# Three token tiles fed together while the weights are decoded, between 24 attention heads and the rest

## The chip, the cores and the metric

The kernel runs on one core of a Trainium2 chip. The metric is the device time of one execution in microseconds. Before the change its median is 1111.67 us over 3 runs (1111.55 to 1111.82).

The core has five engines that work side by side, each through a queue of its own in order: TensorE (PE in the profile: matrix products and transposes, results in the PSUM banks), VectorE (DVE), ScalarE (ACT), GpSimd (POOL) and SyncE (SP, which issues most of the transfers). PEld is TensorE's loading of stationary operands.

## The reference

An attention with a window and 32 global tokens, then a feed-forward layer over all 4608 tokens of the result (8 batches, 8 heads, 512 local and 32 global tokens each, 64 values per head). `sm` is a softmax.

```python
s_g = scale * q_g @ [k_g, k_l].T
out_g = sm(s_g) @ [v_g, v_l]                 # global queries see all keys
s_ll = where(|i - j| <= 32, scale * q_l @ k_l.T, -1e9)
s_lg = scale * q_l @ k_g.T
out_l = sm([s_lg, s_ll]) @ [v_g, v_l]        # local queries: window and global keys
x = concat([out_g, out_l]).reshape(4608, 512)
g = s * relu(x @ w_in) ** 2 + b              # w_in 512 x 2048
return (g @ w_out).astype(float32)           # w_out 2048 x 512
```

`w_in` and `w_out` reach the kernel as float64.

## The kernel before

**Attention** is cut into 128 slots `j`, one for each batch, half of its 512 queries, and head; I call a slot a head. A head has scores (`ps_s`), the scores of the global queries (`ps_g`), a softmax on VectorE, ScalarE and, for some, GpSimd, four transposes (`ps_t`) and the products with the values (`ps_o`). Each of these four PSUM tiles has one bank. Eight heads fill one tile `x` of 256 tokens. The heads 0 to `NF` - 1 are *plain*: float32 operands as they are (`scores32`, `transposes32`, `pv32`). The others are *split*: ScalarE makes a rounded high part, VectorE or GpSimd the low part, and TensorE works on float32r pairs (`split`, `scores`, `pv_products`). The global queries go by groups of four heads (`g_softmax`, `g_transposes`, `g_load`, `g_pv`).

**The feed-forward layer** runs over 17 tiles of 256 tokens (the last has the global ones, by way of DRAM). `x_split` or `xg_split` makes a tile's high and low part, `xs`. A tile has 8 *units*, each with two of the 16 columns of blocks of `w_in`. A unit's first products (`ffn_in`, L494: 24 of 128x256) go to a bank `ps_h`; ScalarE and VectorE make `r` and then `g` in high and low part (L500, L501, L508, L509); its second products (`ffn_out`, L526: 12 of 128x512) are added up over the tile's 8 units in two banks, `acc0` and `acc1`.

**The weights** come in 32 pieces, `w_in` and `w_out` in turn: `weight_piece` puts the words of the float64 together on VectorE (L129, L134, L138, L142), ScalarE (L132, L133, L145) and GpSimd (L144, L146), and leaves a high and a low part in SBUF for good. Unit `pr` of any tile needs the pieces 4 `pr` to 4 `pr` + 3. The list `SPOTS` says in whose buffers a piece is prepared, since no space is kept for it.

**The order** of the work is written out in one loop over `j`: loads for head `j` + 2, up to three weight pieces (`PIECES`, the 32 of them in the first 14 rounds), the scores of head `j`, the first products of unit `m` = `j` - `LAG` with `LAG` = 12, transposes of head `j` - 1 and values of `j` - 2, then the second products of unit `m` - 1. So each slot has one head and one unit, from unit 0 beside head 12; the last 20 slots have units alone or nearly so. A scheduler then places each engine's instructions by this order and by its own times; on the chip each engine keeps that order. With `NF` = 16 the plain heads are those of the first batch.

Of the kernel before, what the change touches and what calls it, by code (L numbers as in the profile page):

```python
# [20 lines left out]
P = 128  # L21
# [27 lines left out]
NORM_POOL = lambda j: j < NF  # L49
# [6 lines left out]
GL_POOL = lambda m: False  # L56
# [9 lines left out]
def window_attention_then_ffn(ctx: ExitStack, tc: tile.TileContext, qd, qg, kw, vw, vg, w_in, w_out, sv, bv, out):  # L66
# [33 lines left out]
    # The weights come as float64: a piece's words are put together as float32, with the exponent  # L100
    # bounded to float32's range (smaller is 0, larger not finite) and the mantissa rounded.
# [3 lines left out]
    def weight_piece(k):  # L105
# [22 lines left out]
        # 2^e with the sign  # L128
# [8 lines left out]
        # 1 + the mantissa: 8 + 20 bits of the high word, less 7, and the low word  # L137
# [54 lines left out]
    def softmax(j, p_s):  # L192
# [45 lines left out]
    def load32(j):  # L238
        b, hf, h = slot(j)
        if h % 2 == 0:  # L240
            if j % 4 == 0:
                rk = sb.tile([P, 480], F32, tag="rk", name=f"rk{j}", bufs=1)
            else:
                rk = sb.tile([P, 10 * D], F32, tag="rvg", name=f"rk{j}", bufs=1)[:, 0:480]
# [41 lines left out]
    # yields after each block's transposes  # L286
# [38 lines left out]
    def qg_load32(b):  # L325
        n = (NF - 16 * b) * SG
# [11 lines left out]
    def scores(j):  # L338
# [14 lines left out]
        # rows of the global queries: qh.k + ql.k  # L353
# [13 lines left out]
    # yields after each block's products  # L367
# [22 lines left out]
    # The last products of a block are shorter than the load of the next values' chunk: transposes go between.  # L390
# [39 lines left out]
    # by pairs of heads  # L430
# [27 lines left out]
    NT = 17  # L458
    xs_ = {}

    def x_split(t):
        xs = sb.tile([P, 2, 4, HALF], F32R, tag="xs", name=f"xs{t}", bufs=1)
        x = xcur.pop(t)
        for i in range(2):
            v = slice(2 * i, 2 * i + 2)
            nc.scalar.copy(out=xs[:, 0, v, :], in_=x[:, v, :])
            nc.vector.tensor_sub(out=xs[:, 1, v, :], in0=x[:, v, :], in1=f32(xs[:, 0, v, :]))
        xs_[t] = xs

    def xg_split(t):  # L470
        xs = sb.tile([P, 2, 4, HALF], F32R, tag="xs", name=f"xs{t}", bufs=1)
        for i in range(2):
# [12 lines left out]
    def ffn_in(m):  # L485
        t, pr = m // 8, m % 8
        xs = xs_[t]
        p_h = ps.tile([P, 2, HALF], F32, tag="h", name=f"ps_h{m}", bufs=2)
        for k in range(2):
            f = 2 * pr + k  # L490
            n = 0
            for c in range(4):
                for a, e in ((0, 0), (0, 1), (1, 0)):
                    nc.tensor.matmul(  # L494
                        p_h[:, k], lhsT=wi[:, a, c, f * P:(f + 1) * P], rhs=xs[:, e, c, :],
# [3 lines left out]
        r = sb.tile([P, 2, HALF], F32, tag="r", name=f"r{m}", bufs=2)  # L499
        nc.scalar.activation(out=r, in_=p_h, func=AF.Relu)  # L500
        nc.vector.scalar_tensor_tensor(out=r, in0=p_h, scalar=s_t, in1=r, op0=ALU.mult, op1=ALU.mult)  # L501
        g = sb.tile([P, 2, 2, HALF], F32R, tag="g", name=f"g{m}")
        if GL_POOL(m):
            nc.vector.tensor_scalar_add(r, r, b_t)
            nc.scalar.copy(out=g[:, 0], in_=r)
            nc.gpsimd.tensor_sub(out=g[:, 1], in0=r, in1=f32(g[:, 0]))
        else:
            nc.scalar.activation(out=g[:, 0], in_=r, func=AF.Identity, bias=b_t)  # L508
            nc.vector.scalar_tensor_tensor(  # L509
                out=g[:, 1], in0=r, scalar=b_t, in1=f32(g[:, 0]), op0=ALU.add, op1=ALU.subtract,  # L510
            )
        gs_[m] = g
# [3 lines left out]
    def ffn_out(m):  # L516
        t, pr = m // 8, m % 8
        g = gs_.pop(m)
        if pr == 0:
            oacc[t] = [ps.tile([P, DM], F32, tag=f"acc{i}", name=f"acc{t}_{i}") for i in range(2)]  # L520
# [25 lines left out]
    NM = NT * 8  # L546
# [12 lines left out]
    def pick(f32_one, split_one):  # L559
        def run(j):  # L560
            if NF <= j < NS:
                split_one(j)
            elif 0 <= j < NF:
                with tc.high_priority(offset=AHEAD):
                    f32_one(j)
        return run

    ld = pick(load32, load)
    sp = pick(lambda j: None, split)
    vl, vl32 = pick(lambda j: None, v_load), pick(v_load32, lambda j: None)  # L570
    sc = pick(scores32, scores)
    tr = pick(transposes32, lambda j: None)
    vsp = pick(lambda j: None, v_split)
    pvs = pick(pv32, lambda j: None)
    piece = 0
# [116 lines left out]
```

## Time and profile before

| | |
|---|---|
| median of 3 runs | 1111.67 us |
| span of the profiled execution, first to last instruction | 1109.8 us |
| time outside the span, median less span | 1.9 us |
| TensorE busy | 1064.7 us, 96% of the span |
| VectorE | 872.3 us, 79% |
| ScalarE | 722.4 us, 65% |
| GpSimd | 426.9 us, 38% |
| transfers | 86.80 MB, 78 GB/s on average |

Of the profiled execution the profile gives the span and no time of its own; the median of the runs stands in for it. The page cuts the span into 40 slices of 27.7 us and gives each engine's busy share in tenths. Timelines give the start and length of instructions in a row; since products overlap in the array, the distance from one start to the next is what a group costs, not its length. The granted clock is the share of TensorE's full clock.

### The profile page before, as it was taken

How to read it: one execution, taken by the hardware profiler on the slowest of the kernel's cores; microseconds unless marked ns; L12 is line 12 of the kernel's file. 1: busy time of each engine (PE TensorE's matmuls, PEld its weight loads, DVE VectorE, ACT ScalarE, POOL GpSimd, SP SyncE). 2: the span in 40 equal slices, each digit the busy share in tenths (PEclk: the TensorE clock that was granted, in tenths of full speed). 3: DMA queues.
4: the chain of work that ended last, by engine and by line, in shares of the span. 5: the costliest groups of instructions: out<-in, count | busy, mean ns of one | idle time of the engine just before them, and what ended most of it. 6: DMA issues, size and time to landing. Idle time of an engine off the chain costs nothing.

```text
span 1109.8 us, 20489 instructions
## 1 busy us (share of the span) xinstructions
PE 1064.7 (96%) x7048; PEld 930.7 (84%) x7048; DVE 872.3 (79%) x2119; ACT 722.4 (65%) x1828; POOL 426.9 (38%) x457
## 2 busy tenths in 40 slices
PE   4889879999999999999999999999999999999996
PEld 2457668889989889898998999989989899998885
DVE  7999998789778977798778977897789777964221
ACT  6666767677667766686767775776678676844221
POOL 6887774343224423343323433442344242411000
PEclk9968999999999999999999999999999999999998
DMA  6454422232213212231223221321223121201000
GB/s 231 149 164 140 153 67 87 69 95 72 63 50 93 77 37 93 66 91 54 82 62 95 67 69 46 106 72 44 78 65 100 45 93 56 85 6 45 20 20 19
DMA packets 63536, 86.80 MB, mean 78 GB/s; under 512 B 7624, under 2 KB 50632, under 8 KB 63432
## 3 DMA queue, kind: packets, MB, share of 16 engines
q1 hardware_dynamic: 63144, 84.44, 24.9%
q8 instruction: 56, 0.92, 0.3%
q10 hardware_dynamic: 288, 1.05, 0.2%
q14 instruction: 48, 0.39, 0.1%
HBM read 76.02 MB, written 9.44 MB: 77 GB/s over the span
## 4 chain that ended last, share of the span: by engine, by line
PE 84%; DVE 12%; issue 1%; DMA 1%; ACT 0%; POOL 0%; DVEq 0%
PE acc L526 33%; PE ps_h L494 32%; PE ps_t L293 7%; PE ps_s L345 4%; PE ps_o L372 4%; DVE we L134 2%; DVE wst L138 2%; DVE we L129 2%; PE ps_og L446 2%; DVE wst L142 2%; PE ps_g L351 1%; DVE g L509 1%; DVE ss L210 1%; DVE sm L201 1%; PE ps_tg L424 1%
## 5 line engine op out<-in xcount | busy, mean ns | idle before, releaser
L494 PE MATMUL ps_h<-xs,wi 128*128 128x256 f32 x3264 | 445.4, 283 | 3.1 <-DVE r L501 2.0
L526 PE MATMUL acc<-wo,g 128*128 128x512 f32 x1632 | 431.1, 399 | 4.9 <-DVE g L509 2.7
L494 PEld LDWEIGHTS ps_h<-xs,wi 128*128 128x128 f32 x3264 | 420.2, 190 | 18.2 <-DVE r L501 2.5
L526 PEld LDWEIGHTS acc<-wo,g 128*128 128x128 f32 x1632 | 289.9, 189 | 59.5 <-DVE g L509 3.6
L189 POOL TENSOR_TENSOR vs<-rv,vs 128x256 fp32r<-128x256 f32 x112 | 94.9, 847 | 221.4 <-ACT vs L188 215.6
L501 DVE SCALAR_TENSOR_TENSOR r<-ps_h,s_t,r 128x512 f32<-128x512 f32 x136 | 101.5, 746 | 70.6 <-ACT r L500 70.1
L508 ACT ACTIVATE g<-r,b_t 128x512 fp32r<-128x512 f32 x136 | 98.2, 722 | 63.4 <-DVE r L501 62.5
L509 DVE SCALAR_TENSOR_TENSOR g<-r,b_t,g 128x512 fp32r<-128x512 f32 x136 | 109.3, 803 | 38.2 <-ACT g L508 36.5
L500 ACT ACTIVATE r<-ps_h 128x512 f32<-128x512 f32 x136 | 81.1, 597 | 85.8 <-PE ps_h L494 77.7
L181 POOL TENSOR_TENSOR kq<-rq,kq 128x256 fp32r<-128x256 f32 x112 | 90.1, 805 | 116.0 <-ACT kq L180 108.6
L207 ACT ACTIVATE sm<-sm,nm 128x224 f32<-128x224 f32 (+1 forms) x256 | 118.5, 467 | 18.1 <-DVE nm L201 17.0
L293 PE MATMUL ps_t<-ident,sm 128*128 128x128 f32 (+2 forms) x512 | 115.5, 291 | 1.4 <-ACT x L316 0.8
L179 POOL TENSOR_TENSOR kq<-rk,kq 64x416 fp32r<-64x416 f32 x56 | 62.0, 1108 | 120.9 <-ACT kq L178 112.5
L201 DVE CUSTOM_DVE_ANT_0 sm<-ps_s,mask 128x224 f32<-128x224 f32 (+1 forms) x256 | 85.2, 366 | 20.3 <-PE ps_t L293 10.8
L293 PEld LDWEIGHTS ps_t<-ident,sm 128*128 128x128 f32 (+2 forms) x512 | 64.9, 143 | 32.1 <-issue 6.1
L438 POOL TENSOR_TENSOR vsg<-rvg,vsg 128x320 fp32r<-128x320 f32 x64 | 58.8, 938 | 84.4 <-ACT vsg L437 84.3
L214 DVE TENSOR_SCALAR sm<-sm,ss 128x192 f32<-128x192 f32 (+1 forms) x224 | 86.8, 430 | 3.4
L372 PE MATMUL ps_o<-pt,vs 128*128 128x256 f32 x448 | 84.5, 284 | 0.0
L345 PE MATMUL ps_s<-kq 128*128 128x192 f32 (+1 forms) x448 | 77.7, 279 | 2.8 <-DVE kq L179 1.2
L345 PEld LDWEIGHTS ps_s<-kq 128*128 128x128 f32 x448 | 67.6, 194 | 9.3 <-DVE kq L179 1.5
L372 PEld LDWEIGHTS ps_o<-pt,vs 128*128 128x128 f32 x448 | 69.8, 195 | 3.1
L361 ACT CAST pt<-ps_t 128x416 fp32r<-128x416 f32 x112 | 57.0, 509 | 15.2 <-PE ps_t L293 14.7
(82 smaller groups left out, 1389.8 us busy)
## 6 DMA issues: line engine op xcount, KB each, us to landing
rq<-in_qd SPq DMA_DIRECT2D x128, 128.0 KB, 2.2
rv<-in_vw SPq DMA_DIRECT2D x128, 128.0 KB, 2.1
rk<-in_kw SPq DMA_DIRECT2D x64, 208.0 KB, 2.4
rvg<-in_vg SPq DMA_DIRECT2D x32, 320.0 KB, 2.9
out<-o SPq DMA_DIRECT2D x34, 256.0 KB, 3.0
wst<-in_w_in SPq DMA_DIRECT2D x15, 512.0 KB, 3.8
wst<-in_w_out SPq DMA_DIRECT2D x15, 512.0 KB, 3.8
rqg<-in_qg SPq DMA_DIRECT2D x8, 128.0 KB, 2.8
```

Of the source, the lines that this page charges most:

```text
L181: nc.gpsimd.tensor_sub(out=qs[:, 1, :], in0=rq, in1=f32(qs[:, 0, :]))
L189: nc.gpsimd.tensor_sub(out=vs[:, :, 1, :], in0=rv4, in1=f32(vs[:, :, 0, :]))
L201: nc.vector.tensor_tensor_reduce(out=sm[:, c], in0=p_s[:, c], in1=mask, op0=ALU.add, op1=ALU.min, scale=-scale, scalar=BIG, accum_out=nm[: ...
L207: nc.scalar.activation(out=p, in_=p, func=AF.Exp, bias=nm[:, blk:blk + 1], scale=-1.0, accum_out=ss[:, blk:blk + 1],)
L293: nc.tensor.transpose(out=p_t[:, o], in_=sm[q, c0:c0 + P], identity=ident[q, q])
L345: nc.tensor.matmul(p_s[:, cols], lhsT=qs[:, a, blk * P:(blk + 1) * P], rhs=ks[:, cols], start=(a == 0), stop=(a == 1),)
L372: nc.tensor.matmul(p_o[:, blk, :, q0:q0 + n], lhsT=vs[:, 2 * blk + c], rhs=pt[:, :, o], start=(c == 1), stop=(c == 0),)
L494: nc.tensor.matmul(p_h[:, k], lhsT=wi[:, a, c, f * P:(f + 1) * P], rhs=xs[:, e, c, :], start=(n == 0), stop=(n == 11),)
L501: nc.vector.scalar_tensor_tensor(out=r, in0=p_h, scalar=s_t, in1=r, op0=ALU.mult, op1=ALU.mult)
L508: nc.scalar.activation(out=g[:, 0], in_=r, func=AF.Identity, bias=b_t)
L509: nc.vector.scalar_tensor_tensor(out=g[:, 1], in0=r, scalar=b_t, in1=f32(g[:, 0]), op0=ALU.add, op1=ALU.subtract,)
L526: nc.tensor.matmul(oacc[t][i], lhsT=g[:, a, k, i * P:(i + 1) * P], rhs=wo[:, e, f, :], start=(pr == 0 and n == 0), stop=(pr == 7 and n == 5),)
```

## The change

Five things change together.

- 32 heads, not 16, are plain (`NF` = 32). Their normalisation is GpSimd's.
- The loop is in stages. The heads 0 to 23 come first, with one weight piece in each of eight rounds (`EARLY_PIECES`). Then the tiles 0, 1 and 2 take units 0 to 5 in turn, (0,0), (1,0), (2,0), (0,1) and so on, with four more pieces in every three units, and no heads. Their units 6 and 7 follow tile by tile, the last two with the heads 24 and 25 beside them. Then come heads without units up to round 33, since tile 3 needs the heads 24 to 31. After that each round has a head and a unit of the tiles 3 to 16, as before.
- Three tiles at once need six banks to add up in: `acc0` and `acc1`, and for the tiles 0 and 1 the banks of `s`, `g`, `t` and `o` (`FIRST_ACC`), which the heads use before and after. So head 24's scores (bank `s`) wait for tile 0's copy to SBUF, and its transposes (bank `t`) for tile 1's.
- `xs` has two buffers, tile 2 takes two of the three `kq` buffers for it, and the load buffer of the keys is doubled. The pieces have other places (`SPOTS`; `n` has a buffer of its own).
- A tile's `x_split` stands at the end of the round that has its last head's values, and its first unit follows in the next round; before, two rounds lay between the two.

```diff
-NF = 16
-AHEAD = 0
-LAG = 12
-SPOTS = (["a","b","c","c","xs"]+["c","c","a","b"]*1+["a","b","c","c"]*12)[:32]
-PIECES = [2, 2, 2, 2, 2, 2, 2, 2, 2, 2, 3, 3, 3, 3]
+NF = 32
+FIRST = 3
+TOGETHER = 6
+FIRST_ACC = {0: ("s", "g"), 1: ("t", "o")}
+SPOTS = ["n", "a", "c", "n", "a", "c", "n", "c"] + ["n", "b", "d", "e"] * 6
+EARLY_PIECES = {2: 1, 5: 1, 8: 1, 11: 1, 14: 1, 17: 1, 20: 1, 22: 1}
...
+        tags = {"a": ("kq", 1024, 3, "vsg", 1280, 1), "b": ("pg", 1280, 1, "pt", 832, 2), "c": ("kq", 1024, 3, "vs", 512, 2),
+                "d": ("vsg", 1280, 1, "vs", 512, 2), "e": ("kq", 1024, 3, "vs", 512, 2), "n": ("ws", 1024, 1, "qgs", 512, 1)}
...
+    def xs_tiles(t):
+        if t == FIRST - 1:
+            xs_[t] = [sb.tile([P, 4, HALF], F32R, tag="kq", name=f"xs{t}_{i}", bufs=3) for i in range(2)]
+        else:
+            xs = sb.tile([P, 2, 4, HALF], F32R, tag="xs", name=f"xs{t}", bufs=2)
+            xs_[t] = [xs[:, i] for i in range(2)]
+        return xs_[t]
...
         if pr == 0:
-            oacc[t] = [ps.tile([P, DM], F32, tag=f"acc{i}", name=f"acc{t}_{i}") for i in range(2)]
+            tags = FIRST_ACC.get(t, ("acc0", "acc1"))
+            oacc[t] = [ps.tile([P, DM], F32, tag=tags[i], name=f"acc{t}_{i}") for i in range(2)]
...
+    def head_and_unit(j, unit=None, heads_until=NS + 9):
...
+        if unit is not None:
+            ffn_in(*unit)
...
+        if unit is not None:
+            if done_units:
+                ffn_out(*done_units[-1])
+            done_units.append(unit)
+        if j in late:
+            late.pop(j)()
+        if j is not None and j % 8 == 1 and 0 <= j // 8 - 1 < 16 and j // 8 - 1 in xcur:
+            x_split(j // 8 - 1)
...
+    H1 = 8 * FIRST
+    for j in range(H1):
+        pieces(EARLY_PIECES.get(j, 0))
+        head_and_unit(j)
+    for j in (H1, H1 + 1):
+        head_and_unit(j, heads_until=H1)
+    for p in range(TOGETHER):
+        for t in range(FIRST):
+            pieces((2, 1, 1)[t] if len(done_pieces) < 32 else 0)
+            head_and_unit(None, (t, p))
+    last = [(t, p) for t in range(FIRST) for p in range(TOGETHER, 8)]
+    j = H1
+    for n, unit in enumerate(last):
+        if n < 4:
+            head_and_unit(None, unit)
+        else:
+            head_and_unit(j, unit)
+            j += 1
+    while j < H1 + 10:
+        head_and_unit(j)
+        j += 1
+    rest = [(t, p) for t in range(FIRST, NT) for p in range(8)]
+    for unit in rest:
+        if unit == (NT - 1, 0):
+            xg_split(NT - 1)
+        head_and_unit(j if j < NS + 10 else None, unit)
+        j += 1
+    ffn_out(*done_units[-1])
```

Where the instructions stand now is decided by the scheduler. Lines of the changed kernel differ by a few from those of before: L494, L526, L267, L273, L293 and L310 of before are L494, L521, L261, L267, L287 and L304 after, and the decoding's L129, L134, L138, L142 are L126, L131, L135, L139. In the rows, the left tile is written and the right ones are read; numbers only tell buffers apart.

The first place is TensorE's queue where the first products of tile 0's unit 0 become ready. Before, around the scores of the twelfth head:

```order
L494 MATMUL ps_h_888<-xs_883,wi 128x256
L494 MATMUL ps_h_989<-xs_883,wi 128x256
L273 MATMUL ps_g_975<-rk_683,rqg_102 32x288
L494 MATMUL ps_h_888<-xs_883,wi 128x256 x17
L494 MATMUL ps_h_989<-xs_883,wi 128x256 x4
L267 MATMUL ps_s_794<-rk_565,rq_625 128x224
```

And after the change, with the first digit behind `ps_h` the unit's number:

```order
L494 MATMUL ps_h_0_1231<-xs_480,wi 128x256
L261 MATMUL ps_s_536<-rk_410,rq_446 128x224
L261 MATMUL ps_s_536<-rk_410,rq_446 128x192
L267 MATMUL ps_g_609<-rk_485,rqg_102 32x288
L287 MATMUL ps_t_506<-ident,sm_453 128x96
L287 MATMUL ps_t_506<-ident,sm_453 128x128
L494 MATMUL ps_h_0_1231<-xs_480,wi 128x256 x15
L287 MATMUL ps_t_506<-ident,sm_453 128x64
L287 MATMUL ps_t_506<-ident,sm_453 128x128
L494 MATMUL ps_h_0_1231<-xs_480,wi 128x256 x2
L267 MATMUL ps_g_667<-rk_568,rqg_102 32x288
```

Before, unit 1 (`ps_h_989`) follows at once and further units after it. Now unit 0 stands alone: of the next first products, tile 1's, six come four heads of scores later, and most of them eight.

The second place is VectorE's queue where the decoding is densest. Before, pieces (`we`, `wst`), units (`r`, `g`) and softmaxes (`ss`, `sm`) are mixed:

```order
L129 TENSOR_SCALAR we_688<-wst_687 128x512
L138 TENSOR_SCALAR wst_639<-wst_639 128x512
L129 TENSOR_SCALAR we_712<-wst_711 128x512
L509 SCALAR_TENSOR_TENSOR g_916<-r_913,b_t,g_916 128x512
L142 SCALAR_TENSOR_TENSOR wst_639<-wst_639 128x512
L501 SCALAR_TENSOR_TENSOR r_1014<-ps_h_989,s_t,r_1014 128x512
L210 TENSOR_SCALAR ss_801<-ss_801 128x2
L134 SCALAR_TENSOR_TENSOR we_688<-wst_687,we_688 128x512
L211 RECIPROCAL ss_801<-ss_801 128x2
```

After, in the stage of the three tiles:

```order
L135 TENSOR_SCALAR wst_1262<-wst_1262 128x512
L504 SCALAR_TENSOR_TENSOR g_1_1428<-r_1_1425,b_t,g_1_1428 128x512
L135 TENSOR_SCALAR wst_1319<-wst_1319 128x512
L139 SCALAR_TENSOR_TENSOR wst_1262<-wst_1262 128x512
L501 SCALAR_TENSOR_TENSOR r_1_1482<-ps_h_1_1457,s_t,r_1_1482 128x512
L139 SCALAR_TENSOR_TENSOR wst_1319<-wst_1319 128x512
L126 TENSOR_SCALAR we_1389<-wst_1388 128x512
L131 SCALAR_TENSOR_TENSOR we_1389<-wst_1388,we_1389 128x512
L135 TENSOR_SCALAR wst_1388<-wst_1388 128x512
L139 SCALAR_TENSOR_TENSOR wst_1388<-wst_1388 128x512
L126 TENSOR_SCALAR we_1446<-wst_1445 128x512
```

The softmaxes are gone from this stretch; pieces and units share VectorE. Of the 32 pieces, 14 stand among the 24 heads and 18 here.

The third place is TensorE's queue behind the last second products of tile 2 (`acc_1_1432`). Before, a head at such a place lay between units:

```order
L494 MATMUL ps_h_2022<-xs_1610,wi 128x256 x13
L446 MATMUL ps_og_2_1635<-vsg_2_1524,pg_0_1256 64x128 x10
L345 MATMUL ps_s_1891<-kq_1766 128x192 x2
L345 MATMUL ps_s_1891<-kq_1766 128x224 x2
L526 MATMUL acc_0_1862<-wo,g_1832 128x512 x2
L526 MATMUL acc_1_1863<-wo,g_1832 128x512
```

After:

```order
L261 MATMUL ps_s_2693<-rk_2584,rq_2621 128x224
L261 MATMUL ps_s_2693<-rk_2584,rq_2621 128x192
L287 MATMUL ps_t_2676<-ident,sm_2628 128x64
L287 MATMUL ps_t_2676<-ident,sm_2628 128x128
L267 MATMUL ps_g_2696<-rk_2584,rqw_662 32x288
L304 MATMUL ps_o_2725<-pt_2681,rv_2653 64x128
L304 MATMUL ps_o_2725<-pt_2681,rv_2653 64x96
L304 MATMUL ps_o_2725<-pt_2681,rv_2653 64x128
L304 MATMUL ps_o_2725<-pt_2681,rv_2653 64x64
```

Here a plain head's pieces follow the pieces of its neighbours with no unit between; the first products of tile 3 start only behind the scores of head 30, six of each of two units at first, and the rest behind the values of head 31.

More of the change, by code (lines that the diff above doesn't have):

```diff
@@ L240, in load32 @@
         if h % 2 == 0:
[L241 to L244, printed above, removed]
+            rk = sb.tile([P, 480], F32, tag="rk", name=f"rk{j}", bufs=2)
             nc.sync.dma_start(rk[:, 0:NC], kw[b, hf, h // 2])
@@ L465, in x_split @@
             v = slice(2 * i, 2 * i + 2)
-            nc.scalar.copy(out=xs[:, 0, v, :], in_=x[:, v, :])
-            nc.vector.tensor_sub(out=xs[:, 1, v, :], in0=x[:, v, :], in1=f32(xs[:, 0, v, :]))
-        xs_[t] = xs
+            nc.scalar.copy(out=hi[:, v, :], in_=x[:, v, :])
+            nc.vector.tensor_sub(out=lo[:, v, :], in0=x[:, v, :], in1=f32(hi[:, v, :]))
     def xg_split(t):
-        xs = sb.tile([P, 2, 4, HALF], F32R, tag="xs", name=f"xs{t}", bufs=1)
+        hi, lo = xs_tiles(t)
         for i in range(2):
@@ L478, in xg_split, with ffn_in @@
             q = slice(i * P, (i + 1) * P)
-            nc.scalar.copy(out=xs[:, 0, :, q], in_=p_t)
-            nc.vector.tensor_sub(out=xs[:, 1, :, q], in0=p_t, in1=f32(xs[:, 0, :, q]))
-        xs_[t] = xs
+            nc.scalar.copy(out=hi[:, :, q], in_=p_t)
+            nc.vector.tensor_sub(out=lo[:, :, q], in0=p_t, in1=f32(hi[:, :, q]))
     gs_ = {}
-    def ffn_in(m):
-        t, pr = m // 8, m % 8
+    def ffn_in(t, pr):
         xs = xs_[t]
-        p_h = ps.tile([P, 2, HALF], F32, tag="h", name=f"ps_h{m}", bufs=2)
+        p_h = ps.tile([P, 2, HALF], F32, tag="h", name=f"ps_h{t}_{pr}", bufs=2)
         for k in range(2):
@@ L563, in run @@
             elif 0 <= j < NF:
-                with tc.high_priority(offset=AHEAD):
-                    f32_one(j)
-        return run
-    ld = pick(load32, load)
-    sp = pick(lambda j: None, split)
-    vl, vl32 = pick(lambda j: None, v_load), pick(v_load32, lambda j: None)
-    sc = pick(scores32, scores)
[L572 to L575, printed above, removed]
+                f32_one(j)
+        return run
@@ new lines, in once, with run @@
+    def once(fn):
+        seen = set()
+        def run(j):
+            if j not in seen:
+                seen.add(j)
+                fn(j)
+        return run
+    ld = once(pick(load32, load))
+    sp = once(pick(lambda j: None, split))
+    vl, vl32 = pick(lambda j: None, v_load), once(pick(v_load32, lambda j: None))
+    sc = pick(scores32, scores)
+    tr = once(pick(transposes32, lambda j: None))
+    vsp = once(pick(lambda j: None, v_split))
+    pvs = once(pick(pv32, lambda j: None))
@@ new lines, in window_attention_then_ffn, with pieces @@
+    split_stages = once(lambda j: transposes_and_pv(j - 1, j - 2))
+    done_pieces, done_units = [], []
+    def pieces(n):
+        for _ in range(n):
+            weight_piece(len(done_pieces))
+            done_pieces.append(None)
+    def head_and_unit(j, unit=None, heads_until=NS + 9):
+        if j is not None:
+            if j < min(heads_until, NS):
+                sp(j + 1)
+                ld(j + 2)
+                vl(j)
+                b1 = j // 16 + 1
+                if j == 14 and NF > 16:
+                    qg_load32(1)
+                elif j % 16 == 14 and b1 < B and j + 2 >= NF:
+                    qg_load(b1)
+                sc(j)
+                if j % 16 == 15 and NF <= j + 1 < NS:
+                    qg_split(b1)
+            if j in early:
+                early.pop(j)()
+        if unit is not None:
+            ffn_in(*unit)
+        if j is not None:
+            if j - 1 < heads_until:
+                tr(j - 1)
+                split_stages(j)
+                vsp(j - 1)
+            for fn in extra.pop(j, []):
+                fn()
+            pvs(j - 2)
+            if j < heads_until:
+                vl32(j)
+        if unit is not None:
[6 more added lines that the diff above has]
+            x_split(j // 8 - 1)
```

98 lines of the change are left out of this document (20 added, 78 removed).

## Prediction

> **What bounds the kernel now.** I read the page's slices first, then the state at 300 us, then the timeline of TensorE before and after 90 us, then its clock.
>
> ```profile
> PE   4889879999999999999999999999999999999996
> PEld 2457668889989889898998999989989899998885
> DVE  7999998789778977798778977897789777964221
> ```
>
> A slice is 27.7 us. VectorE is full from the second to the sixth, where the weights are decoded; from the seventh on TensorE is full and stays so. The kernel is thus a front part of some 170 us, in which TensorE has gaps, and a saturated remainder, in which nothing but TensorE's work counts. A change of the front part is worth what it does to the moment from which TensorE is full, with equal work left. So I price a state, not single instructions.
>
> ```profile
> core 0 of [0], span 1109.8 us
> 0.00:300.00 300.00, 91.47 (x632) 84.99 (x633) 0.95 0.37 117
> 0.00:300.00 300.00, 77.37 (x288) 51.33 (x288) 0.95 0.37 117
> 0.00:300.00 300.00, 14.81 (x84) 12.61 (x84) 0.95 0.37 117
> ```
>
> These are the windows of the first 300 us for L494, L526 and L345 alone. The count in brackets is what matters: 632 first products (24 make a unit, so 26.3 units), 288 second products (12 make a unit, so 24 units) and the scores of 84/4 = 21 split heads, 37 heads with the 16 plain ones.
>
> ```profile
> 1077.78 2.96 PE L526 MATMUL acc<-wo,g 128*128 128x512 f32 x12
> 1080.58 2.96 PE L494 MATMUL ps_h<-xs,wi 128*128 128x256 f32 x24
> 1083.37 2.96 PE L526 MATMUL acc<-wo,g 128*128 128x512 f32 x12
> ```
>
> Between starts, a unit's first products cost 2.79 us (0.117 each) and its second 2.80 (0.233 each): 5.6 us a unit at full clock.
>
> **A plain head at two clocks.** The change doubles the plain heads, so their price on TensorE is the next number.
>
> ```profile
> 48.05 1.65 PE L310 MATMUL ps_o<-pt,rv 128*64 128x128 f32 x8 [0.59 <-ACT pt L301]
> 49.62 0.77 PE L293 MATMUL ps_t<-ident,sm 64*128 64x64 f32 x2
> 50.33 1.75 PE L267 MATMUL ps_s<-rk,rq 64*128 64x192 f32 x4
> 52.01 0.63 PE L293 MATMUL ps_t<-ident,sm 96*128 96x96 f32 x2
> 52.57 1.17 PE L273 MATMUL ps_g<-rk,rqg 64*32 64x288 f32 x2
> 53.67 0.79 PE L494 MATMUL ps_h<-xs,wi 128*128 128x256 f32 x2
> ```
>
> Start to start, a head costs 1.57 for its values (L310), 1.27 for four transposes (L293), 1.68 for scores (L267) and 1.10 for the global scores (L273): 5.6 us, with no gap between them.
>
> ```profile
> 109.69 0.67 PE L273 MATMUL ps_g<-rk,rqg 64*32 64x288 f32 x2
> 110.29 1.32 PE L494 MATMUL ps_h<-xs,wi 128*128 128x256 f32 x9
> 111.54 0.64 PE L267 MATMUL ps_s<-rk,rq 64*128 64x224 f32 x2
> 112.12 0.87 PE L293 MATMUL ps_t<-ident,sm 96*128 96x96 f32 x4
> 112.92 0.93 PE L310 MATMUL ps_o<-pt,rv 128*64 128x128 f32 x8
> 113.78 0.59 PE L267 MATMUL ps_s<-rk,rq 64*128 64x192 f32 x2
> ```
>
> Sixty us later the same pieces cost 0.60, 1.10 (two halves), 0.80 and 0.86: 3.4 us. The clock makes the difference:
>
> ```profile
> 71.84:75.25 3.41, 3.41 (x11) 0.50 0.22 67
> 85.49:88.90 3.41, 3.41 (x15) 0.50 0.51 159
> 95.73:99.14 3.41, 3.41 (x18) 1.00 0.61 168
> 146.92:150.33 3.41, 1.40 (x6) 1.00 0.15 38
> 150.33:153.75 3.42, 3.42 (x14) 0.50 0.00 0
> ```
>
> Window, its length, TensorE's busy time, then the granted clock. At 71.84 TensorE is busy without a gap, with plain heads alone, and the clock stays at 0.50. It opens after this run of first products:
>
> ```profile
> 83.25 4.85 PE L494 MATMUL ps_h<-xs,wi 128*128 128x256 f32 x21
> ```
>
> It falls back after a window with 1.40 us of work (146.92). At 95.73, heads with a few second products between them hold it. So plain heads don't open the clock; whether heads alone would hold it, no row shows.
>
> The Trainium skill (TensorE: Matmul & The Clock Gate, Part 1: The HAM clock gate) says that the array runs at half rate by default and at full rate after one busy window of some 3.4 us. The row at 71.84 is such a window at 0.50, so for plain heads the trace doesn't bear the rule out; by the rule the time would be the one that the third rival below works out.
>
> **The change in four stages.** I count TensorE's work in the order of the changed program; everything else lies beside it unless I say so.
>
> *Stage A: to the end of the first products of tile 0's unit 0.* In the order these stand behind 12 score pairs, 14 global scores, 10 sets of transposes and 9 of values. At half clock: 12 x 1.68 + 14 x 1.10 + 10 x 1.27 + 9 x 1.57 = 62.4 us, and 24 first products at 4.78/21 = 0.228 are 5.5.
>
> ```profile
> PE ps_g L273 <- DMA rk<-in_kw: 10.6, 1, 10.6
> ```
>
> TensorE starts at 10.6 us, as before. For early waits I add 5: the first two slices of before leave 6 to 12 us unused of the 45 after the start, with more decoding between the heads; the ends are 0 and 12. A = 10.6 + 62.4 + 5.5 + 5 = 83.5 us. By the rows shown the clock doesn't open sooner, as only six of the first products stand earlier in the queue.
>
> *Stage B: the rest of 24 heads.* 12 scores, 10 global scores, 14 transposes, 15 values are 72.6 us at half clock and 43.3 at full; 72 first products (8.4), 24 second ones (5.6) and the global queries' pieces of the first batch (4, an estimate from their columns) are 18. Ends: 61 and 91 or more. I let a quarter of the head work, next to the three groups of first products, run at full clock: 65 + 18 = 83. VectorE has only 14 of the 32 pieces to decode by the end of B and isn't late there; what it gains lies beside TensorE's slower work.
>
> *Stage C: three tiles together.* 480 first and 264 second products, with head 24's scores: 56 + 61.6 + 1.5 = 119 us. VectorE:
>
> ```profile
> L134 DVE SCALAR_TENSOR_TENSOR we<-wst,we 128x512 int32<-128x512 int32 x31 | 30.8, 996 | 1.3 <-ACT we L132 1.2
> L142 DVE SCALAR_TENSOR_TENSOR wst<-wst 128x512 f32<-128x512 f32 x32 | 27.9, 875 | 0.3
> L129 DVE TENSOR_SCALAR we<-wst 128x512 int32<-128x512 int32 x31 | 26.8, 867 | 6.0 <-DMA wst<-in_w_in 6.0
> L138 DVE TENSOR_SCALAR wst<-wst 128x512 int32<-128x512 int32 x32 | 25.7, 809 | 0.2
> L210 DVE TENSOR_SCALAR ss<-ss 128x2 f32<-128x2 f32 x22 | 12.0, 547 | 0.5 <-ACT sm L207 0.2
> L509 DVE SCALAR_TENSOR_TENSOR g<-r,b_t,g 128x512 fp32r<-128x512 f32 x11 | 11.9, 1084 | 0.1
> L201 DVE CUSTOM_DVE_ANT_0 sm<-ps_s,mask 128x224 f32<-128x224 f32 x22 | 8.3, 379 | 0.0
> L501 DVE SCALAR_TENSOR_TENSOR r<-ps_h,s_t,r 128x512 f32<-128x512 f32 x11 | 8.1, 739 | 0.5 <-ACT r L500 0.4
> ```
>
> A piece is 0.996 + 0.875 + 0.867 + 0.809 = 3.55 us, a unit 1.08 + 0.74 = 1.82. In VectorE's order 18 pieces, three low parts (L509's 1.08 each) and 12 units stand up to the last piece: 64 + 3 + 22 = 89 us, against 12 x 5.6 = 67 on TensorE. The units behind it can't make this up, as TensorE is full there. Of the 22 us I take 14, since TensorE still has attention work of stage B when the first of these pieces starts. Ends: 0, and 40 if a piece takes 4.6 us (the 31 pieces of before lay between 6.8 and 147.7 us, all other VectorE work included). C = 133.
>
> The added bank waits (head 24's scores behind tile 0's output copy, head 24's transposes behind tile 1's) cost nothing here: a whole unit, 5.6 us, stands in TensorE's queue between the tile's last product and the waiting instruction. If the copy came later than that, TensorE would stop, as its queue is in order. SP's queue carries each piece's load ahead of later heads' loads; the pieces of this stage have three places, so a late place delays all that is behind it. That is in the upper end of C.
>
> *Stage D: the heads that tile 3 waits for.* Tiles 0 to 2 are used up and tile 3 needs heads 24 to 31, so 6 scores, 6 global scores, 8 transposes and 8 values stand nearly bare: 39.5 us at half clock, 23.5 at full, and 4 of split scores and first products. Before, such heads lay between units. D = 40 for a clock that falls soon after the last second products; ends 27 and 47.
>
> Sum: 83.5 + 83 + 133 + 40 = 339.5 us.
>
> **What is left then.** 24 units are done, 12 first products of tile 3, heads 0 to 31 whole and three more scored: against before at 300 us that is 44 first products (5 us), two heads' worth (3) and some global pieces (2) less, so the state of before at about 290. From there before needs 1109.8 - 290 = 820 us, and the changed order leaves the same work: 339.5 + 820 = 1159.5 us span. The median lies 1.9 above the span (1111.67 against 1109.8): **1161 us**. In the remainder a tile's split now stands right before its first unit, where two units lay between; the tile's second buffer and 6 us of other queued TensorE work cover it, so I cost it at 0 (at most 1 us for each of 13 tiles).
>
> **Rivals.**
> *Heads hold the clock.* It opens with tile 0's first unit and stays: A 83.5, B 61, C 133, D 28, 305 us, so 1127. For it: 95.73. Against: that window had second products in it, B and D have stretches without. Chance 0.22.
> *Decoding sets the pace of C.* Each piece at 4.6 us: 26 more than forecast, 1187. For it: the three places of the pieces; against: GpSimd has fewer other tasks there. Chance 0.10.
> *Any busy TensorE opens the clock (the other side).* A's heads have fewer pieces between them than before; if the clock opens at about 31 us, A is 10.6 + 20 + two thirds of the same work at full clock (28) + 5 = 64, B 61, C with little waiting 124, D 27: 276, so 1098. It decides when the sum is below 288. Against it: the row at 71.84. Chance 0.08.
> *The work only changes places,* with the sum near 290: 1111. Chance 0.04.
> The forecast itself, 1145 to 1172: 0.56.
>
> **Numbers.** Slower by over 0.2% (about what a measurement of this kernel tells from none): 0.56 + 0.22 + 0.10 = 0.88; within: 0.04; faster: 0.08. The range goes from a little below the first rival's 1127, at 1120, to 1180, which takes in A, B and D's ends and half of C's.
>
> **What would show it.** Right: first units' products near 78 to 84 us; clock 0.50 in most windows of plain heads, also of 24 to 31; the last L131 near 255; TensorE full from about 340 with no gaps at tile bounds. Wrong: a clock of 1.00 before 75 us or through heads 12 to 23 (B at 61), or stage C without waits on VectorE; if TensorE is full with 24 units done before 288 us, the sign is wrong.

## The result, and the profile after

The changed kernel takes **1147.49 us** (median of 4 runs, 1146.2 to 1151.42); the kernel before, run on the same chip, 1111.61 (1111.31 to 1111.82). The ratio is 1.0329, with a 95% interval of 1.0312 to 1.0346: slower by 36 us. 1161 was predicted, with a range of 1120 to 1180.

From the page of the profile after: TensorE's line of busy time, and two rows of the 40 slices (28.6 us each).

```profile
span 1144.3 us, 20456 instructions
PE 1094.9 (96%) x7128; PEld 944.8 (83%) x7128; DVE 807.7 (71%) x2015; ACT 707.7 (62%) x1779; POOL 389.8 (34%) x448
PE   6898987899999999999999999999999999999996
DVE  7645489932477887788777977798778976884321
```

Two things are to be seen. VectorE is no longer full from the second slice to the sixth, but in the sixth to the eighth alone, the stage of three tiles. And TensorE's busy time went from 1064.7 to 1094.9 us, by 30.2, while its unused time (span less busy) went from 45.1 to 49.4, by 4.3. So most of the 34.5 us of span is busy time and not waiting.

The windows of the changed kernel, cut where the prediction's stages A to D and the remainder end. After the length stand the busy times of PE, PEld, DVE, ACT and POOL with their counts, then the granted clock, the share of the transfers and GB/s.

```profile
0.00:80.30 80.30, 66.07 (x212) 40.64 (x212) 47.91 (x123) 43.34 (x107) 46.95 (x58) 1.00 0.46 146
80.30:146.40 66.10, 60.47 (x391) 45.06 (x390) 35.69 (x121) 46.75 (x130) 26.21 (x39) 0.97 0.46 137
146.40:231.00 84.60, 68.27 (x398) 58.86 (x397) 82.10 (x97) 47.73 (x79) 52.69 (x36) 0.96 0.34 99
231.00:284.80 53.80, 53.80 (x339) 46.97 (x338) 16.26 (x32) 16.87 (x32) 1.71 (x4) 1.00 0.09 29
284.80:322.10 37.30, 34.57 (x194) 23.87 (x192) 16.57 (x71) 26.40 (x76) 12.27 (x20) 0.96 0.32 90
322.10:1144.30 822.20, 811.75 (x5603) 729.40 (x5603) 609.15 (x1574) 526.66 (x1358) 249.99 (x292) 0.99 0.22 64
```

The third and fourth row are stage C: VectorE is busy for 82.10 of 84.60 us while TensorE leaves 16.3 unused; then VectorE has decoded everything, and TensorE works without a gap. The clock of the first row isn't to be taken as it stands: it reads 1.00 although the durations in it are those of half clock, since the record begins with its first change, the opening at 80.5 us. Below are the window from 47 us on, TensorE's timeline around the end of stage A, and the two windows ahead of the next fall of the clock:

```profile
47.00:80.30 33.30, 33.30 (x117) 22.55 (x116) 13.23 (x49) 15.44 (x43) 12.20 (x16) 1.00 0.32 95
...
66.21 1.65 PE L304 MATMUL ps_o<-pt,rv 128*64 128x128 f32 x8
75.72 3.55 PE L494 MATMUL ps_h<-xs,wi 128*128 128x256 f32 x15
82.71 0.93 PE L304 MATMUL ps_o<-pt,rv 128*64 128x128 f32 x8
93.64 0.97 PE L494 MATMUL ps_h<-xs,wi 128*128 128x256 f32 x6
...
101.00:104.41 3.41, 2.64 (x15) 1.69 (x15) 1.06 (x7) 1.95 (x8) 1.95 (x3) 1.00 0.61 208
104.41:107.82 3.41, 1.97 (x10) 1.31 (x10) 2.52 (x9) 3.31 (x9) 0.00 (x0) 1.00 0.39 101
```

From 47 to 80.3 TensorE has no gap, and yet a head's values still take 1.65 us at 66; from 82 on they take 0.93. The clock opens right behind the first products at 75.72, and then stays open until 107.8. From 80.5 to 93.6 TensorE has plain heads alone; then come the six first products at 93.64 and a few transposes of the global queries. The clock outlasts a window with 2.64 us of work, and falls behind one with 1.97.

### The profile page after: what moved, and what is told of

It reads as the page before. It is cut to its first block, busy times and chain, and to the rows that moved or that the text cites. A ratio compares the mean times of both kernels' runs of the same rounds, so it can differ in the third digit from the quotient of the medians.

```text
span 1144.3 us, 20456 instructions
## 1 busy us (share of the span) xinstructions
PE 1094.9 (96%) x7128; PEld 944.8 (83%) x7128; DVE 807.7 (71%) x2015; ACT 707.7 (62%) x1779; POOL 389.8 (34%) x448
## 4 chain that ended last, share of the span: by engine, by line
PE 85%; DVE 8%; DMA 3%; ACT 2%; issue 1%; POOL 0%; SPq 0%; POOLq 0%; DVEq 0%; ACTq 0%
PE ps_h L494 31%; PE acc L521 31%; PE ps_t L287 7%; PE ps_s L339 4%; PE ps_o L366 3%; PE ps_o L304 2%; PE ps_s L261 2%; DVE we L131 2%; PE ps_og L440 2%; DVE wst L139 1%; DVE wst L135 1%; PE ps_g L267 1%; DMA wst<-in_w_in 1%; DVE we L126 1%; PE ps_g L345 1%
## 5 line engine op out<-in xcount | busy, mean ns | idle before, releaser
L494 PE MATMUL ps_h<-xs,wi 128*128 128x256 f32 x3264 | 444.2, 284 | 4.4 <-DVE r L501 2.5
L521 PE MATMUL acc<-wo,g 128*128 128x512 f32 x1632 | 429.6, 401 | 13.8 <-DVE g L504 9.1
L494 PEld LDWEIGHTS ps_h<-xs,wi 128*128 128x128 f32 x3264 | 418.6, 191 | 19.1 <-DVE r L501 2.8
L521 PEld LDWEIGHTS acc<-wo,g 128*128 128x128 f32 x1632 | 292.6, 190 | 73.7 <-DVE g L504 11.3
L504 DVE SCALAR_TENSOR_TENSOR g<-r,b_t,g 128x512 fp32r<-128x512 f32 x136 | 114.9, 845 | 52.1 <-ACT g L503 49.0
L186 POOL TENSOR_TENSOR vs<-rv,vs 128x256 fp32r<-128x256 f32 x96 | 74.1, 771 | 164.2 <-ACT vs L185 164.0
L198 DVE CUSTOM_DVE_ANT_0 sm<-ps_s,mask 128x224 f32<-128x224 f32 (+1 forms) x256 | 85.3, 368 | 55.1 <-PE ps_t L287 33.4
L287 PE MATMUL ps_t<-ident,sm 128*128 128x128 f32 (+2 forms) x512 | 114.1, 293 | 5.1 <-DVE gs L405 1.4
L178 POOL TENSOR_TENSOR kq<-rq,kq 128x256 fp32r<-128x256 f32 x96 | 79.3, 826 | 103.3 <-ACT kq L177 96.8
L287 PEld LDWEIGHTS ps_t<-ident,sm 128*128 128x128 f32 (+2 forms) x512 | 64.8, 145 | 40.9 <-issue 8.2
L176 POOL TENSOR_TENSOR kq<-rk,kq 64x416 fp32r<-64x416 f32 x48 | 53.8, 1120 | 124.0 <-ACT kq L175 111.3
L366 PE MATMUL ps_o<-pt,vs 128*128 128x256 f32 (+2 forms) x384 | 71.1, 282 | 0.0
L211 POOL TENSOR_SCALAR sm<-sm,ss 128x192 f32<-128x192 f32 (+1 forms) x64 | 33.4, 534 | 106.0 <-DVE ss L208 82.9
L141 POOL TENSOR_TENSOR we<-wst,we 128x512 f32<-128x512 f32 x32 | 46.9, 1466 | 57.2 <-DVE wst L139 27.9
L339 PE MATMUL ps_s<-kq 128*128 128x224 f32 (+1 forms) x384 | 65.4, 278 | 0.0
L211 DVE TENSOR_SCALAR sm<-sm,ss 128x192 f32<-128x192 f32 (+1 forms) x192 | 62.0, 365 | 2.9
L380 DVE TENSOR_TENSOR x<-u 64x256 f32<-64x256 f32 x96 | 58.6, 610 | 3.1
```

The source lines that it names most:

```text
L198: nc.vector.tensor_tensor_reduce(out=sm[:, c], in0=p_s[:, c], in1=mask, op0=ALU.add, op1=ALU.min, scale=-scale, scalar=BIG, accum_out=nm[: ...
L211: (nc.gpsimd if j < NF else nc.vector).tensor_scalar(out=p, in0=p, scalar1=ss[:, blk:blk + 1], scalar2=1.0, op0=ALU.mult, op1=ALU.mult,)
L287: nc.tensor.transpose(out=p_t[:, o], in_=sm[q, c0:c0 + P], identity=ident[q, q])
L339: nc.tensor.matmul(p_s[:, cols], lhsT=qs[:, a, blk * P:(blk + 1) * P], rhs=ks[:, cols], start=(a == 0), stop=(a == 1),)
L366: nc.tensor.matmul(p_o[:, blk, :, q0:q0 + n], lhsT=vs[:, 2 * blk + c], rhs=pt[:, :, o], start=(c == 1), stop=(c == 0),)
L494: nc.tensor.matmul(p_h[:, k], lhsT=wi[:, a, c, f * P:(f + 1) * P], rhs=xs[e][:, c, :], start=(n == 0), stop=(n == 11),)
```

## The experiments

**Theory 1, the heads' work:** the change costs what 16 more plain heads cost TensorE, about 2 us each, and the new order itself neither wins nor loses. **Theory 2, the order:** the time is lost in the new stages: half clock in A, waits for decoded weights in C, heads without units in D. Each run below stands against the kernel before on the same chip (medians of 1111.2 to 1111.5 us). Where an edit changes the program, its scheduler also lays neighbouring instructions anew, so differences of a few us are not read.

### The old order with 32 and with 24 plain heads

```diff
-NF = 16
+NF = 32
-            rk = sb.tile([P, 480], F32, tag="rk", name=f"rk{j}", bufs=1)[:, 0:NC]
+            rk = sb.tile([P, 480], F32, tag="rk", name=f"rk{j}", bufs=2)[:, 0:NC]
...
-        n = (NF - 16 * b) * SG
+        n = min(NF - 16 * b, H) * SG
```

The second kernel is the same with `NF = 24`.

> The kernel of before, its order unchanged, with 32 plain heads instead of 16 (and the buffers that this needs); nothing else of the change. Theory 1 (the heads' work): the change costs time because 16 more heads run as plain float32 products, 3.4 us of TensorE each at full clock against about 1.4 us split, so about 2 us for each head that runs where TensorE is full: 1127 to 1143 us, 15 to 31 us above before, most of the 36 us that the change costs. Theory 2 (the order): the time is lost to the changed order, to the half clock of its first 80 us, to the waits for decoded weights while three tiles run together and to the heads without units behind them: this kernel has none of these, so 1112 to 1120 us.

> The kernel of before with 24 plain heads instead of 16, nothing else of the change. With 32 it took 1147.7 us, 36 us above before. Theory 1 (each plain head costs TensorE about 2.3 us more than a split one, where TensorE is full): half of that, 1127 to 1131 us. Rival: the 36 us come from somewhere else in that kernel (a clock that falls, a late load of the keys in the second batch), so that they don't go with the number of heads: below 1118 or above 1140 us.

Measured: 1147.69 us with 32 plain heads (1147.51 to 1148.25; ratio 1.0327, 1.0312 to 1.0343) and 1127.43 with 24 (ratio 1.0146, 1.0129 to 1.0163). Span and TensorE's busy time from the page of the first:

```profile
span 1145.7 us, 20487 instructions
PE 1105.8 (97%) x7128; PEld 942.4 (82%) x7128; DVE 820.0 (72%) x2015; ACT 709.5 (62%) x1779; POOL 403.6 (35%) x448
```

The old order with the heads of the new one takes as long as the changed kernel, 1147.7 against 1147.5, without any of the new stages. The cost goes with the number of heads: 16.0 us for the first eight (2.0 each), 20.3 for the next (2.5 each). Theory 1's upper end, 1143, was still 5 us low. With 32 plain heads TensorE's busy time rises by 41.1 us, and its unused time falls by 5.2 (45.1 to 39.9). So the new order is a draw in time. But it isn't without effect: against this kernel it has 10.9 us less busy time (1105.8 to 1094.9) and 9.5 more unused (39.9 to 49.4).

The timeline shows one thing that the new order saves. TensorE of the old order with 32 plain heads, where it is full, at full clock; the last four rows are a split head's values with its transposes, its scores, and what follows each:

```profile
213.37 0.48 PE L523 MATMUL acc<-wo,g 128*128 128x512 f32 x1
213.78 0.43 PE L307 MATMUL ps_o<-pt,rv 128*64 128x128 f32 x2
214.15 0.50 PE L523 MATMUL acc<-wo,g 128*128 128x512 f32 x1
214.58 0.33 PE L307 MATMUL ps_o<-pt,rv 128*64 128x64 f32 x2
214.84 0.50 PE L523 MATMUL acc<-wo,g 128*128 128x512 f32 x1
...
409.53 0.37 PE L369 MATMUL ps_o<-pt,vs 128*128 128x256 f32 x2
...
410.49 3.03 PE L523 MATMUL acc<-wo,g 128*128 128x512 f32 x12
413.36 0.60 PE L342 MATMUL ps_s<-kq 128*128 128x192 f32 x4
...
413.92 1.81 PE L491 MATMUL ps_h<-xs,wi 128*128 128x256 f32 x14
```

The same work in the changed kernel's stage D, where heads stand in blocks:

```profile
288.35 0.97 PE L261 MATMUL ps_s<-rk,rq 64*128 64x224 f32 x4
289.25 0.67 PE L267 MATMUL ps_g<-rk,rqw 64*32 64x288 f32 x2
289.85 0.87 PE L287 MATMUL ps_t<-ident,sm 96*128 96x96 f32 x4
290.66 0.93 PE L304 MATMUL ps_o<-pt,rv 128*64 128x128 f32 x8
291.52 2.84 PE L521 MATMUL acc<-wo,g 128*128 128x512 f32 x11
```

In a block, eight products with the values cost 0.86 us from start to start, two of them 0.22, and a second product costs 0.23 (2.80 for twelve, in the prediction's rows): 0.45 for the pair. Taken in turns, the pair costs 0.78 (213.37 to 214.15) and 0.69 (214.15 to 214.84). In the two traces, a product with a plain head's values is followed by a second product 26 times in the old order with 32 plain heads, and 3 times in the changed kernel; at 0.24 to 0.33 us each, that makes 6 to 8 of the 10.9 us (an estimate). The rest is open, and no run tried it by itself. A plain head in a block is 3.17 us (288.35 to 291.52), a split one 1.52 (0.96 from 409.53 to 410.49, 0.56 from 413.36 to 413.92). So the products of 16 heads make some 26 us of the 36, and the turns most of the rest (both estimates).

### The new order with 24 plain heads

```diff
-NF = 32
+NF = 24
...
-        if n < 4:
-            head_and_unit(None, unit)
-        else:
-            head_and_unit(j, unit)
-            j += 1
+        head_and_unit(None, unit)
+    qg_load(1)
+    qg_split(1)
+    sp(H1)
+    ld(H1 + 1)
```

> The changed kernel with heads 24 to 31 split as before the change (24 plain heads); their eight rounds stand without units behind the six last units of tiles 0 to 2. Theory 1: eight heads at about 2 us less on TensorE each, so 15 us less: 1130 to 1135 us. Theory 2: these eight heads are bare, and a split head has more work on VectorE and ScalarE (about 4 us each) than a plain one; their stage doesn't get shorter: 1145 to 1160 us.

Measured: 1158.74 us, the median of three runs (1157.34 to 1160.08; ratio 1.0426, 1.0408 to 1.0443), 11 us above the changed kernel; a fourth run took 2042.9 us, which no trace explains, and isn't counted. Theory 1 fails here with its sign; theory 2's range held. Windows of this kernel's stage D, and TensorE's longest wait in it:

```profile
286.00:306.00 20.00, 14.32 (x64) 10.86 (x63) 15.91 (x55) 14.04 (x41) 7.64 (x10) 0.72 0.29 82
306.00:326.00 20.00, 14.72 (x62) 12.22 (x61) 18.42 (x54) 14.82 (x45) 9.42 (x13) 0.51 0.26 75
```

```profile
PE ps_s L339 <- DVE nm L198: 5.6, 5, 1.5
```

Without units between them split heads run near VectorE's pace (15.91 and 18.42 of 20 us); TensorE has gaps, the clock falls to 0.51, and even the little work left takes twice as long. The loss lies in this stage: the clock opens for the rest at 339.1 us, in the changed kernel at 326.3, and what follows is 812 us at full clock in both. So these eight plain heads are a price of the order: it puts heads 24 to 31 where nothing covers them, and there plain heads are the cheaper kind. The edit also takes heads 24 and 25 from beside the last two units, so a part of the loss may be theirs. Theory 1 is right on the sum, and theory 2 on why the new order, as it is, is no faster with eight plain heads fewer. The new order was not run with 16.

### Lighter decoding, in the new order and in the old

```diff
-        nc.vector.scalar_tensor_tensor(
-            out=e, in0=high, scalar=-(1 << 31), in1=e, op0=ALU.bitwise_and, op1=ALU.bitwise_or,
-        )
...
-        nc.vector.tensor_scalar(
-            out=high, in0=high, scalar1=0xFFFFF, scalar2=0x41000000, op0=ALU.bitwise_and, op1=ALU.bitwise_or,
-        )
```

> The changed kernel with two of the four VectorE operations of each weight piece left out (those that take the sign and the mantissa), so that the weights come out wrong; a piece costs VectorE about 1.7 us instead of 3.4. If VectorE's decoding sets the pace of the stage in which three tiles run together, its some 14 to 16 us of waits go: 1129 to 1134 us. If the waits there come from somewhere else (the loads of the pieces, GpSimd's low parts, the units' own chain through ScalarE and VectorE), the time stays within 5 us of the changed kernel's 1147.

> The kernel of before with the same two VectorE operations of each weight piece left out (sign and mantissa; the weights come out wrong), some 55 us less work on VectorE in its first 160 us, where it is 97% busy. If before's front is bound by decoding more than the changed one is, it gains more than the changed kernel did (7 us in the median, 15 in its profiled run): 1085 to 1097 us; then the changed order does shorten what decoding costs, and gives the gain back in its own stages. If before's front is bound by its heads' chain and the half clock as much, it gains no more than 10 us: 1101 to 1108, and there was little for the order to win.

Measured: the new order 1140.88 us (1132.75 to 1147.98; ratio 1.0263, 1.0205 to 1.0320), the old one 1095.20 (1093.36 to 1097.48; ratio 0.9856, 0.9837 to 0.9875). Stage C with its tail, and TensorE's waits, first in the changed kernel, then in the new order with lighter decoding, cut at the same count of products (its lines stand six lower: L515, L498, L497, L488 and L495), with two rows of its timeline:

```profile
144.00:268.00 124.00, 107.67 (x647) 94.11 (x646) 93.58 (x113) 58.54 (x95) 52.69 (x36) 0.97 0.25 75
...
PE acc L521 <- DVE g L504: 9.1, 7, 1.8
PE acc L521 <- ACT g L503: 4.6, 4, 1.8
PE ps_h L494 <- DVE r L501: 2.5, 1, 2.5
```

```profile
136.00:253.50 117.50, 106.42 (x647) 94.02 (x647) 72.88 (x77) 57.25 (x95) 52.79 (x36) 0.97 0.26 80
...
PE acc L515 <- DVE g L498: 4.3, 3, 1.7
PE ps_h L488 <- DVE r L495: 3.9, 1, 3.9
PE acc L515 <- ACT g L497: 2.8, 2, 2.1
...
48.40 1.65 PE L488 MATMUL ps_h<-xs,wi 128*128 128x256 f32 x6
52.19 0.93 PE L298 MATMUL ps_o<-pt,rv 128*64 128x128 f32 x8
```

The stage gets 6.5 us shorter, not 16: the waits fall from 16.2 to 11.0 us, though VectorE's busy time there falls by 20.7. What the 11 us still wait for in the end, no run shows. Another 8 us come from the stages ahead, which have pieces too. There the clock opens behind the six first products at 48.40, so that a head's values take 0.93 us at 52; it falls again at 60. The same six, at 47.27 in the changed kernel, don't open it. The fastest of the new order's four runs is 15 us below the changed kernel and the slowest equal to it; where the slow ones lose it, no trace shows. The median is thus between the two cases that were expected. The old order, in its range, gains 16 us, and the new one 7 in the median and 15 at most: the new order may pay less for decoding, but the wait for VectorE has moved from the first 160 us into stage C and is not gone.

### Decoding more of it early

```diff
-SPOTS = ["n", "a", "c", "n", "a", "c", "n", "c"] + ["n", "b", "d", "e"] * 6
-EARLY_PIECES = {2: 1, 5: 1, 8: 1, 11: 1, 14: 1, 17: 1, 20: 1, 22: 1}
+SPOTS = ["n", "c", "c"] * 6 + ["n", "c"] + ["n", "b", "d", "e"] * 3
+EARLY_PIECES = {j: 1 for j in range(2, 22)}
...
-            pieces((2, 1, 1)[t] if len(done_pieces) < 32 else 0)
+            pieces((1, 1, 0)[t] if len(done_pieces) < 32 else 0)
```

> The changed kernel with 20 pieces of the weights decoded beside the first 24 heads instead of 8, one in each round from 2 to 21, and 12 instead of 24 in the stage of three tiles (the buffers of the pieces chosen to suit). If VectorE's decoding is what that stage waits for, its waits of some 15 us go, as in the run with lighter pieces, and the VectorE time that the heads' stages leave unused pays for it: 1130 to 1137 us. If decoding beside the heads delays them as much (their softmax stands behind the pieces in VectorE's queue): 1142 to 1152 us.

Measured: 1145.77 us (1138.03 to 1150.85; ratio 1.0305, 1.0257 to 1.0354), in the second of the two ranges and not to be told from the changed kernel. Its stages A, B and C with the tail, in the fastest of the runs:

```profile
0.00:84.00 84.00, 67.22 (x216) 40.93 (x216) 70.44 (x152) 55.84 (x131) 63.82 (x67) 1.00 0.58 184
84.00:152.00 68.00, 60.53 (x373) 43.39 (x372) 45.08 (x127) 49.10 (x132) 42.17 (x49) 0.92 0.45 137
152.00:262.00 110.00, 104.02 (x641) 92.37 (x641) 59.00 (x76) 41.65 (x68) 27.80 (x18) 0.98 0.13 41
```

The mechanism was right: the last row is 110 us, where the changed kernel needs 124, and TensorE's waits in it are 6.0 us instead of 16.2. But the heads' stages end at 152 where they ended at 144. VectorE's unused time there isn't free: TensorE's waits for the softmax (L198, L269, L295) rise from 5.1 to 10.3 us, and the second row's clock is 0.92. 8 of 14 us go back even in this run.

### Opening the clock

Products that nobody reads, at the very start of the new order and of the old, and then (new order) behind head 6:

```diff
+    warm = const.tile([P, 256], BF16, name="warm")
+    nc.vector.memset(warm, 1.0)
+    p_w = ps.tile([P, 2, HALF], F32, tag="h", name="ps_w", bufs=2)
+    for _ in range(48):
+        nc.tensor.matmul(p_w[:, 0], lhsT=warm[:, 0:P], rhs=warm, start=True, stop=True)
```

```diff
         head_and_unit(j)
+        if j in (6,):
+            warm = sb.tile([P, 256], BF16, tag="warm", name=f"warm{j}", bufs=1)
+            nc.vector.tensor_copy(out=warm, in_=st_["p", j][:, 0:256])
+            p_w = ps.tile([P, 2, HALF], F32, tag="h", name=f"ps_w{j}", bufs=2)
+            for _ in range(32):
+                nc.tensor.matmul(p_w[:, 0], lhsT=warm[:, 0:P], rhs=warm, start=True, stop=True)
```

> The changed kernel with 48 bfloat16 products on a constant tile ahead of the first head, into a PSUM bank that nobody reads, in time that TensorE waits for the first loads anyway. If dense products open the clock and plain heads then hold it, as they held it from 80 us on, the first stage (80 us in the changed kernel, its heads at half clock) takes 50 to 60 us: 1120 to 1128 us. If the heads of the first stage let the clock fall, or are bound by their loads and softmax instead of the clock: within 5 us of 1147.

> The kernel of before with 48 bfloat16 products on a constant tile ahead of its first head. In the changed kernel these opened the clock and it fell at the first gap, 13 us after the start. If the same happens here: 1109 to 1112 us, no difference that counts. If TensorE's half clock is what holds before's front back and an open clock lasts longer here: 1095 to 1105 us.

> The changed kernel with 32 bfloat16 products of 128x256 behind head 6's softmax (about 50 us, where TensorE has no gaps but half clock), into a bank that nobody reads; their operand is a copy of head 6's probabilities, so that they can't move ahead. If plain heads hold an open clock as long as TensorE has no gaps, the clock opens at about 54 us and stays: the 5 us of products are paid, some 25 us of heads at half clock become 15 to 17, and the first stage ends 4 to 8 us sooner: 1139 to 1144 us. If plain heads let the clock fall even without gaps, it falls within 7 us of the products and the time is 1148 to 1152 us.

> The changed kernel with both: 20 pieces early and the products behind head 6. If both losses are TensorE's own and independent, the gains add: 1123 to 1133 us, still above before, since the 16 more plain heads remain. If with more pieces between them the heads have gaps, the clock falls again behind the products, and the time is that of the run with 20 early pieces, plus up to 5 us.

Measured: at the start of the new order 1144.46 us (ratio 1.0307, 1.0275 to 1.0338), at the start of the old one 1116.81 (1.0044, 1.0028 to 1.0061), behind head 6 1147.59 (1.0326, 1.0310 to 1.0341), and this with 20 early pieces 1155.45 (1.0379, 1.0334 to 1.0424). None wins. The first is in the second of its two ranges, the run behind head 6 between its two; the last is above both cases expected of it, and so is the old order with products at its start. Windows of the new order with products at its start:

```profile
6.82:10.23 3.41, 2.83 (x24) 1.97 (x21) 2.48 (x6) 2.39 (x4) 0.02 (x1) 1.00 1.03 348
9.59:13.00 3.41, 2.03 (x8) 0.89 (x8) 3.34 (x5) 1.31 (x3) 1.70 (x2) 1.00 0.96 277
13.64:17.05 3.41, 2.62 (x6) 1.20 (x6) 2.39 (x8) 2.84 (x9) 2.08 (x3) 0.50 1.01 379
```

The clock is open at 7 us and falls at 13.0, behind a window with 2.03 us of work. Behind head 6 it holds longer; timeline and windows of that run:

```profile
54.92 4.58 PE L635 MATMUL ps_w<-warm 128*128 128x256 bf16 x32
59.43 0.93 PE L304 MATMUL ps_o<-pt,rv 128*64 128x128 f32 x8
70.78 1.68 PE L494 MATMUL ps_h<-xs,wi 128*128 128x256 f32 x12
81.43 0.93 PE L304 MATMUL ps_o<-pt,rv 128*64 128x128 f32 x8 [0.65 <-ACT pt L295]
83.89 0.88 PE L267 MATMUL ps_g<-rk,rqw 64*32 64x256 f32 x2 [0.63 <-DMA rk<-in_kw]
```

```profile
80.69:84.10 3.41, 2.13 (x14) 1.60 (x14) 1.60 (x10) 2.44 (x7) 0.85 (x2) 1.00 0.83 267
85.33:88.75 3.42, 2.54 (x8) 1.61 (x8) 2.53 (x8) 2.18 (x7) 0.00 (x0) 0.50 0.00 0
```

The 32 products open the clock, and a head's values take 0.93 from 59 to 79 us; the 24 first products of tile 0's unit 0 stand between these heads, twelve of them at 70.78. Then the heads have outrun what feeds them, the transposed probabilities (L295) and the keys of the second batch; a window with 2.13 us of work follows, and at 84.1 the clock falls. What stage A won, some 6 us, stage B gave back: the 588 products that the changed kernel has done by 144 us are done by 145.5 here. So here the half clock isn't a loss that can be taken away alone: at full clock the heads wait, and behind the waits the clock falls. Each of the two cases was half right: the clock opened and held without gaps, but the gaps came. That the old order loses 5.6 us by the products at its start wasn't expected; there TensorE is busy for 29.18 us from 20 to 60, where it was 34.30 before. Why is open.

## Why the prediction was right on the whole, and where it failed

The sign and the size held: 1161 against 1147.5, inside the range. The front part was to end at 339.5 us and ended at 322.1; the remainder was to take 820 and took 822.2, so the state that was priced was the right one. That the total is only 13.5 us off owes something to luck, as errors of both signs meet in it. By its steps:

- **Stage A**, 83.5: measured 80.3. The half clock through all of it, the opening by the first unit's products and the 5 us of early waits hold (14.2 us unused, 9.6 of them ahead of the first product). That six first products wouldn't open the clock was not safe to say, as they did in the run with lighter decoding. And in the kernel before it had opened once ahead of the run at 83.25, behind ten first products at 59.73: the next head's values, at 61.95, took 0.93 us, those at 70.68 took 1.65 again.
- **Stage B**, 83: measured 66.1. This is the step that failed: "I let a quarter of the head work, next to the three groups of first products, run at full clock". The clock was 0.97 on average. Plain heads alone held the open clock from 80.5 to 93.6 us, with gaps of 0.38 and 0.69, as the first rival said; the row at 95.73 us of the kernel before was the better witness. Its 61 for this stage is 5 off. A clock of 1.00 through heads 12 to 23 was on the prediction's own list of signs of being wrong.
- **Stage C**, 133: in the prediction's count, with all second products of the three tiles, 138.4 + 5.6 = 144. VectorE is busy for 82.10 of 84.60 us there, and 16.3 us unused on TensorE stand against 14 forecast. That decoding is the bound, the runs show in part: with 12 pieces fewer in the stage 6.0 us of waits are left, with lighter pieces 11.0. The rest of the error is TensorE's own work: 122 us busy and the 5.6, against 119. The window's clock of 0.96 makes some 3.4 us of it (84.6 x 0.04, an estimate), and the others are open.
- **Stage D**, 40: measured 37.3 with those 5.6 of second products in it, so 31.7. Again the clock held, 0.96.
- **Costs set to nothing:** the bank waits and the tile's split. Stage C's tail is busy for 53.80 of 53.80 us, and the remainder is 2 us over. Both hold.

Sum of the errors: -3.2, -16.9, +11.0 and -8.3 make -17.4, less 2.2 more in the remainder. The first rival, 1127, had B and D nearly right, and was 11 us short in C. The prediction also didn't say plainly what the 36 us are. It told of clocks and waits. The old order with 32 plain heads has none of the new stages, leaves less of TensorE unused than before the change (39.9 us against 45.1), and is as slow as the new one.

The Trainium skill (TensorE: Matmul & The Clock Gate, Part 1: The HAM clock gate) has half rate come back after at least one idle window of some 3.4 us. The run with products behind head 6 doesn't agree: there the clock fell behind 3.41 us of which TensorE was busy for 2.13, so the window wasn't idle. The section on HAM oscillation on that page of the Trainium skill has waits for transfers, each long enough to cross such a window, bring the half rate back again and again. The waits ahead of the fall behind head 6 were shorter, 0.65 and 0.63 us.

## What to carry to other kernels

Ask first what work an order forces on the engine that is full afterwards: give the old order the same work, and the rest of the difference is what the order itself does. Here 16 more plain heads cost the old order 36 us, and the new order, which has them, is 36 us slower too. A wait that is removed from one stage, or a clock that is opened in one, is worth only what the next stage doesn't need: 14 us won in the stage of three tiles and 6 in the first stage were given back by half or whole to their neighbours.

## What the runs showed of the hardware

- Plain float32 heads alone held an open clock in the changed kernel from 80.5 to 93.6 us, with two gaps of 0.38 and 0.69 us. With first products between them they held it until 107.8, and until 84.1 in the run with 32 bfloat16 products behind head 6. It fell behind 3.41 us with 1.97, 2.13 and 2.03 us of work in three runs, and outlasted 2.64. Busy time alone doesn't decide: among units it outlasted 1.67 (176.1 to 179.5 in the changed kernel).
- The same heads didn't open it. In the changed kernel TensorE had no gap for 33.3 us, from 47.0 to 80.3, at first with heads and seven first products, and the clock opened only behind fifteen more in a row at 75.72. In the run with lighter decoding six of them, at 48.40, were enough.
- Small products with the values in turns with large second products cost 0.69 to 0.78 us a pair, against 0.45 when each kind stands together.
